# Rotary attention and dense experts on one core: the first pair's second queries rotated on GpSimd, its second keys turned two score tiles later, the third pair loaded sooner

## The chip, the cores and the metric

One core of a Trainium2 chip runs the whole kernel: five engines (TensorE, VectorE, ScalarE, GpSimd, and SyncE, which here only issues transfers) work on one program each and wait for one another by semaphores. In the rows TensorE is PE (its weight loads PEld), VectorE is DVE, ScalarE is ACT, GpSimd is POOL and SyncE is SP. The metric is the device time of one execution in microseconds (us), the median of the runs.

## What is computed

```python
def _attn_ref(q, k, v):                      # (2, 8, 576, 64) each
    ...
    def rotate(x):
        x1, x2 = (x[..., :half], x[..., half:])
        return np.concatenate([x1 * cos - x2 * sin, x1 * sin + x2 * cos], axis=-1)
    q_rot, k_rot = (rotate(q), rotate(k))
    scale = 1.0 / np.sqrt(D)
    scores = scale * np.matmul(q_rot, k_rot.transpose(0, 1, 3, 2))
    ...
    return np.matmul(attn, v)                # attn: softmax of the scores

def _moe_ref(x, domain_probs, w1, w2):       # x (1152, 512), 4 experts, all used by every token
    p = domain_probs / (domain_probs.sum(-1, keepdims=True) + 1e-09)
    for e in range(E):
        h = np.maximum(x @ w1[e], 0.0)
        out += p[:, e:e + 1] * (h @ w2[e])
```

Queries and keys are rotated, the softmax attention of 16 heads (2 batches, 8 heads) gives 1152 tokens of 512 features, and these go through four dense experts.

## The kernel before

All products are made of high and low halves in fp32r (a value and its rounding remainder), so every rotated tensor is split in two.

**Pairs and units.** Heads are worked two at a time, a pair: `first` holds the four pairs of batch 0, `second` those of batch 1. A pair's 2 x 576 queries make nine score tiles of 128 rows, the units u = 0 to 8: four of the pair's first head, four of its second, and one (`TAIL`) of the last 64 rows of both. For a unit TensorE makes a score tile `sc` (L281), VectorE takes its maximum `mx` (L292), ScalarE the exponential `e` (L300), TensorE turns `e` into `pp` (L314) and its end into `x` (L340), ScalarE and VectorE copy it as high and low part `ptH`, `ptL`, `ptX` (L331, L335, L343, L347), and every second unit TensorE multiplies with the values (L364 to L367). At a pair's end VectorE inverts the sums `total` (L381, L382), scales the last `e` (L386) and spreads the sums (`rep`, L391), which TensorE turns into `pr` (L397).

**What a pair needs first.** `load` brings raw keys, queries and values (SyncE queue, for the first pair's queries ScalarE's). `rotate` is six instructions on one engine: a product (L184), two half-width products (L188), their sum (L192), and the split into high part (L136 or L140) and low part (L141) of `hl`. `turn_heads` turns a head's rotated keys or queries on TensorE into a bank (`tpk`, `tpq`, L230), `keep_heads` copies the bank to `kT` or `qT` on ScalarE (L235), `turn_tails` and `keep_tails` do the last 64 rows (L253, L265), and `swap` makes the keys' other half `k2T` by two transfers (L245, L246). The first pair's first keys get `k2T` without a transfer.

**Banks.** Score tiles, and the turned heads unless another place is given, take the two `s` banks by turns: a tile can be written once the one before the last has been read.

**Order.** The program is in manual order: each engine runs its instructions as the Python code emits them. The first statements are emitted straight, the rest stands in `plan`, an agenda of due times in units: pair n begins at 9n, `ALONE` gives each step's offset, `FIRST_TURNS` and `TURNS` when the heads of the first and the next pair are turned and kept. Rotations of the third pair on are `jobs`: each half unit, `work(1)` emits one step of the oldest. After 44.5 units the experts of chunk 0 start, with batch 1's pairs between them, then the experts of chunk 1.

**Around the change.** The first pair's first head is rotated at once (keys on VectorE, queries on GpSimd). Then GpSimd rotates the second pair's keys and queries and splits its values, while VectorE rotates the first pair's second keys and then the second queries `pr.rotate("q", ...)` (256 columns, the split at 1.5 units). Buffers come from two pools by turns, `evens` for the first and third pair, `odds` for the second and fourth; the third pair's raw keys can be loaded once the first pair's have been read.

Of the kernel before, what the change touches and what calls it, by code (L numbers as in the profile page):

```python
# [15 lines left out]
F32R = mybir.dt.float32r  # L16
# [31 lines left out]
        tails=(5.299, 5.657), swap=5.707,  # L48
    ),
]  # L50
FIRST_TURNS = dict(q0=(1.327, 1.797), q1=(1.739, 1.84), q_tails=(-0.037, 0.16), swap=0.18)
NEXT_TURNS = dict(tails=(-0.01, -0.008), k=(0.03, 0.056), q=(0.975, 1.004))


# [1 line left out]
def kernel(  # L56
# [17 lines left out]
    nc = tc.nc  # L74
    B, H, S, D = q.shape
    NT, DM = out.shape
    E, _, FF = w1.shape
# [5 lines left out]
    NS = NR + 1  # L83
# [3 lines left out]
    NC = 2 * NR + 1  # L87
# [56 lines left out]
    class Pair:  # L144
# [60 lines left out]
        def turn(self, which, i):  # L205
            return self.hl[which][:, i].rearrange("p two d -> p (two d)")
# [250 lines left out]
    class Weights:  # L457
# [35 lines left out]
        def next(self):  # L493
            self.load()
            self.split()
# [126 lines left out]
    def dst(c, hp, a, z):  # L622
        return xH[c][:, hp, a:z], xL[c][:, hp, a:z]
# [6 lines left out]
    def pools(name, **kw):  # L630
        return [
            attn.enter_context(tc.tile_pool(name=f"{name}0", bufs=1, side="right", **kw)),
            spare.enter_context(tc.tile_pool(name=f"{name}1", bufs=1, **kw)),
        ]

    apool = attn.enter_context(tc.tile_pool(name="apool", bufs=1, side="right"))
    evens, odds = pools("pair")
    banks = {t: Banks(t, pools(t, space=PSUM)) for t in ("s", "pp")}
    banks["pt"] = Banks("pt", pools("pt"))
    xb = [p.tile([P, 512], F32, name=f"x{i}") for i, p in enumerate(pools("x", space=PSUM))]  # L640
# [4 lines left out]
    first = [  # L645
        Pair(0, hp, (evens, odds)[hp % 2], dst(0, hp, 0, SM), dst(1, hp, SM, S)) for hp in range(NP)
    ]
# [31 lines left out]
    plan = Agenda()  # L679
# [5 lines left out]
    def tails(t, pr, *args):  # L685
        plan.at(t[0], lambda: pr.turn_tails(*args))
        plan.at(t[1], lambda: pr.keep_tails(*args))


    pr, nx = first[0:2]  # L690
# [21 lines left out]
    pr.keep_heads("k", (0,), True)  # L712
    pr.keep_tails("k", True)
    pr.split_v(nc.scalar)
    nx.rotate_now("k", nc.gpsimd)
    nx.rotate_now("q", nc.gpsimd)
    nx.split_v()
    pr.rotate_now("k", nc.vector, NS, NC)
    rest = pr.rotate("q", nc.vector, NS, NC)
    for _ in range(3):  # L720
        next(rest)
    plan.at(1.5, lambda: next(rest))
    pr.turn_heads("k", (1,))
    pr.keep_heads("k", (1,))
    turn(FIRST_TURNS["q0"], pr, "q", (0,), False, (2, NR))
    turn(FIRST_TURNS["q1"], pr, "q", (1,))
    tails(FIRST_TURNS["q_tails"], pr, "q")
    plan.at(FIRST_TURNS["swap"], lambda pr=pr: pr.swap(1, 2))


    def load_qk(t, pr):
        def rotate():
            jobs.append(pr.rotate("k", nc.gpsimd))
            jobs.append(pr.rotate("q", nc.gpsimd))

        plan.at(t, lambda: pr.load("k"), lambda: pr.load("q"), rotate)

    def load_v(t, pr):
        plan.at(t, lambda: pr.load("v"), later(pr.split_v))
# [6 lines left out]
    for hp, pr in enumerate(first):  # L746
# [3 lines left out]
        if hp + 1 < NP:  # L750
# [5 lines left out]
                if key in t:  # L756
                    tails(shift(n, t[key]), nx, parts)
            plan.at(n + t["swap"], nx.swap)
    load_qk(7.2, first[2])
    load_v(U + 5.8, first[2])  # L760
    load_qk(U + 0.05, first[3])
    load_v(2 * U + 5.8, first[3])
# [92 lines left out]
```

## Time and profile before

| | |
|---|---|
| time, median of 3 runs | 593.22 us (590.82 to 593.9) |
| the profiled execution's own time | 592.81 us |
| its span, first to last instruction | 590.8 us |
| TensorE busy (matmul) | 559.1 us (95%) |
| VectorE, ScalarE, GpSimd busy | 236.3, 256.0, 279.4 us |
| mean granted TensorE clock | 0.993 |

Attention of batch 0 fills about the first 110 us of the span, the experts with batch 1's attention and then the experts alone the rest. The rows further down are from three views: the order of time (start, duration, engine, line, output<-input; in brackets the idle time before it and what ended it), and a table of stretches with TensorE's busy time and its granted clock, where 1.00 is the level of 2.4 GHz and 0.50 that of 1.2 GHz.

### The profile page before, as it was taken

Reading aid. Unit: us, or ns where it says so; the run is one execution under the profiler, and the core shown is the slowest. Engines: PE = TensorE matmul, PEld = TensorE weight load, DVE = VectorE, ACT = ScalarE, POOL = GpSimd, SP = SyncE. Lnnn points to the kernel's source line nnn. Section 1 sums busy time; section 2 is a strip of 40 time slices with the busy share of each in tenths; the row PEclk is TensorE's granted clock in tenths of the full one; section 3 lists DMA queues with packets and bytes.
Section 4 is the critical chain, followed back from the end, with each engine's and each line's share of the span. In section 5 each row is a group of like instructions: output and inputs, shape, how many; then the busy total and the mean of one; then the engine's idle time right before and its main releaser. Section 6 shows DMA issues by size and latency. Waiting matters only on the chain.

```text
span 590.8 us, 8478 instructions
## 1 busy us (share of the span) xinstructions
PE 559.1 (95%) x3325; PEld 493.6 (84%) x3325; DVE 236.3 (40%) x411; ACT 256.0 (43%) x505; POOL 279.4 (47%) x191
## 2 busy tenths in 40 slices
PE   3788889899999999999999999999999999999997
PEld 2677778688888888888888888998998899889985
DVE  6786889424363434444334542210321042022202
ACT  4685798365444545455535542331232133113300
POOL 7939993267933784378333343333334333333300
PEclk9998999899999999999999999999999999999999
DMA  5052232055126222432252113323222222322002
GB/s 153 15 156 69 71 99 59 0 150 182 36 72 175 71 65 54 124 119 65 72 134 73 60 52 112 96 82 100 71 73 72 71 72 73 101 76 72 0 1 89
DMA packets 40345, 48.57 MB, mean 82 GB/s; under 512 B 7154, under 2 KB 29938, under 8 KB 40306
## 3 DMA queue, kind: packets, MB, share of 16 engines
q1 hardware_dynamic: 39506, 47.28, 27.3%
q10 hardware_dynamic: 800, 0.75, 0.5%
q8 instruction: 26, 0.43, 0.3%
q14 instruction: 13, 0.11, 0.1%
HBM read 41.24 MB, written 2.36 MB: 74 GB/s over the span
## 4 chain that ended last, share of the span: by engine, by line
PE 82%; DVE 8%; ACT 5%; DMA 2%; issue 1%; POOL 1%; SPq 0%; ACTq 0%; DVEq 0%; POOLq 0%
PE po L546 11%; PE po L548 11%; PE po L547 11%; PE ph L567 11%; PE ph L568 11%; PE ph L569 11%; PE sc L281 5%; PE pp L314 4%; PE x L415 3%; ACT e L300 2%; DVE mx L292 2%; PE x L364 2%; PE x L365 2%; DMA rawk<-in_k_dram 1%; PE x L340 1%
## 5 line engine op out<-in xcount | busy, mean ns | idle before, releaser
L141 POOL TENSOR_TENSOR wl<-wr,wh 128x1024 fp32r<-128x1024 f32 x64 | 153.8, 2403 | 237.8 <-ACT wh L134 237.8
L567 PE MATMUL ph<-xH,wh 128*128 128x320 f32 (+1 forms) x384 | 130.6, 340 | 0.0
L569 PE MATMUL ph<-xH,wl 128*128 128x320 f32 (+1 forms) x384 | 129.3, 337 | 0.0
L568 PE MATMUL ph<-xL,wh 128*128 128x320 f32 (+1 forms) x384 | 129.2, 336 | 0.0
L546 PE MATMUL po<-wh,hH 128*128 128x512 f32 x288 | 114.6, 398 | 0.0
L134 ACT ACTIVATE wh<-wr 128x1024 fp32r<-128x1024 f32 x64 | 67.6, 1056 | 105.7 <-PE po L548 79.0
L548 PE MATMUL po<-wh,hL 128*128 128x512 f32 x288 | 112.5, 391 | 0.0
L547 PE MATMUL po<-wl,hH 128*128 128x512 f32 x288 | 112.4, 390 | 0.0
L532 DVE SCALAR_TENSOR_TENSOR hL<-ph,hH 128x320 fp32r<-128x320 f32 (+1 forms) x96 | 51.7, 558 | 145.4 <-ACT hH L531 145.4
L531 ACT ACTIVATE hH<-ph 128x320 fp32r<-128x320 f32 (+1 forms) x96 | 46.8, 491 | 109.1 <-PE ph L569 106.7
L569 PEld LDWEIGHTS ph<-xH,wl 128*128 128x128 f32 x384 | 72.1, 188 | 5.2
L567 PEld LDWEIGHTS ph<-xH,wh 128*128 128x128 f32 x384 | 72.1, 188 | 4.8
L568 PEld LDWEIGHTS ph<-xL,wh 128*128 128x128 f32 x384 | 72.2, 188 | 4.5
L292 DVE TENSOR_REDUCE mx<-sc 128x1 f32<-128x576 f32 x72 | 54.1, 752 | 38.8 <-PE sc L281 38.3
L300 ACT ACTIVATE e<-sc,mx 128x576 f32<-128x576 f32 x72 | 53.3, 740 | 27.4 <-DVE mx L292 26.7
L548 PEld LDWEIGHTS po<-wh,hL 128*128 128x128 f32 x288 | 54.1, 188 | 11.7
L546 PEld LDWEIGHTS po<-wh,hH 128*128 128x128 f32 x288 | 54.1, 188 | 11.2
L547 PEld LDWEIGHTS po<-wl,hH 128*128 128x128 f32 x288 | 54.2, 188 | 10.1
L577 DVE SCALAR_TENSOR_TENSOR acc<-po,probs,acc 128x512 f32<-128x512 f32 x27 | 18.8, 751 | 80.7 <-PE po L548 80.7
L314 PE MATMUL pp<-ident,e 128*128 128x128 f32 x288 | 45.3, 281 | 5.8 <-DVE e L386 3.0
L331 ACT ACTIVATE ptH<-pp 128x512 fp32r<-128x512 f32 x64 | 38.1, 595 | 27.2 <-PE x L364 17.0
L335 DVE TENSOR_TENSOR ptL<-pp,ptH 128x512 fp32r<-128x512 f32 x64 | 43.8, 685 | 9.6 <-ACT ptH L331 9.0
(103 smaller groups left out, 676.7 us busy)
## 6 DMA issues: line engine op xcount, KB each, us to landing
wr<-in_moe_w_dram SPq DMA_DIRECT2D x64, 512.0 KB, 3.5
k2T<-kT SPq DMA_DIRECT2D x14, 288.0 KB, 3.9
rawv<-in_v_dram SPq DMA_DIRECT2D x8, 256.0 KB, 2.9
out_dram<-acc SPq DMA_DIRECT2D x8, 256.0 KB, 3.2
rawk<-in_k_dram SPq DMA_DIRECT2D x7, 256.0 KB, 3.9
rawq<-in_q_dram SPq DMA_DIRECT2D x7, 256.0 KB, 3.1
rawv<-in_v_dram SPq DMA_DIRECT2D x16, 32.0 KB, 2.6
tabs<-in_rope_dram ACTq DMA_DIRECT2D x1, 320.0 KB, 3.5
```

The lines of the kernel that those rows point to most:

```text
L134: nc.scalar.activation(out=hi, in_=src, func=AF.Copy)
L141: eng_l.tensor_tensor(out=lo, in0=src, in1=f32(hi), op=ALU.subtract)
L292: nc.vector.tensor_reduce(out=mx, in_=self.sc[u][:, :, 0:HALF], op=ALU.max, axis=AX.XY, negate=True)
L300: nc.scalar.activation(out=e.rearrange("p (i c) -> p i c", i=2), in_=self.sc.pop(u)[:, :, 0:HALF], func=AF.Exp, bias=self.mx.pop(u), accum ...
L314: nc.tensor.transpose(pp[:, c * P : (c + 1) * P], self.e[u][:, c * P : (c + 1) * P], ident)
L532: nc.vector.scalar_tensor_tensor(out=tL[:, a:z], in0=o, scalar=0.0, in1=f32(tH[:, a:z]), op0=ALU.max, op1=ALU.subtract,)
L546: nc.tensor.matmul(po[t], lhsT=sH, rhs=wH, start=(f == 0), stop=False)
L547: nc.tensor.matmul(po[t], lhsT=sH, rhs=wL, start=False, stop=False)
L548: nc.tensor.matmul(po[t], lhsT=sL, rhs=wH, start=False, stop=(f == NF - 1))
L567: nc.tensor.matmul(o, lhsT=wH[:, kt], rhs=xh, start=(kt == 0), stop=False)
L568: nc.tensor.matmul(o, lhsT=wH[:, kt], rhs=xl, start=False, stop=False)
L569: nc.tensor.matmul(o, lhsT=wL[:, kt], rhs=xh, start=False, stop=(kt == KT1 - 1))
```

## The change

Three things are edited.

- The first pair's second queries (256 columns) are rotated on GpSimd, ahead of the second pair's keys, with the `odds` pool's scratch tiles, instead of on VectorE with those of `evens`. They are turned at 2.3 instead of 1.739 units and kept at 2.5 instead of 1.84.
- The first pair's second keys are turned at 1.1 and kept at 1.3 units, behind two score tiles, instead of ahead of the first; they go through the bank `xb[1]` and no longer through an `s` bank. Their swap is issued at 1.4 instead of 0.18 units. The third and fourth tiles of the first queries are kept at 1.45 instead of 1.797.
- The third pair's keys and queries are loaded, and their rotations queued, at 2.6 instead of 7.2 units.

```diff
-FIRST_TURNS = dict(q0=(1.327, 1.797), q1=(1.739, 1.84), q_tails=(-0.037, 0.16), swap=0.18)
+FIRST_TURNS = dict(q0=(1.327, 1.45), q1=(2.3, 2.5), q_tails=(-0.037, 0.16), swap=1.4)
...
     pr.split_v(nc.scalar)
+    pr.rotate_now("q", nc.gpsimd, NS, NC, odds)
     nx.rotate_now("k", nc.gpsimd)
     nx.rotate_now("q", nc.gpsimd)
     nx.split_v()
     pr.rotate_now("k", nc.vector, NS, NC)
-    rest = pr.rotate("q", nc.vector, NS, NC)
-    for _ in range(3):
-        next(rest)
-    plan.at(1.5, lambda: next(rest))
-    pr.turn_heads("k", (1,))
-    pr.keep_heads("k", (1,))
+    plan.at(1.1, lambda pr=pr: pr.turn_heads("k", (1,), tp=xb[1].bitcast(F32R).unsqueeze(1)))
+    plan.at(1.3, lambda pr=pr: pr.keep_heads("k", (1,)))
...
-    load_qk(7.2, first[2])
+    load_qk(2.6, first[2])
```

TensorE in the opening, before (`sc_0_0` is the first pair's score tile 0, `tpk_0` its second keys, `tpq_0` queries, first the third and fourth tiles of the first head, then the second head):

```order
L230 MATMUL tpk_0_238<-identr,hlk_00_149 128x128 x4
L281 MATMUL sc_0_0_245<-kT_0_185,qT_0_188 128x288 x2
L281 MATMUL sc_0_0_245<-k2T_0_197,qT_0_188 128x288 x2
L253 MATMUL tlq_00_250<-identr,hlq_00_158 128x128
L281 MATMUL sc_0_1_259<-kT_0_185,qT_0_188 128x288 x2
L281 MATMUL sc_0_1_259<-k2T_0_197,qT_0_188 128x288 x2
L230 MATMUL tpq_0_266<-identr,hlq_00_158 128x128 x2
L314 MATMUL pp_0_0_269<-ident,e_0_0_257 128x128 x4
L230 MATMUL tpq_0_281<-identr,hlq_00_158 128x128 x4
L281 MATMUL sc_0_2_287<-kT_0_185,qT_0_188 128x288 x2
```

and now (`x_113` is the bank `xb[1]`):

```order
L281 MATMUL sc_0_0_241<-kT_0_185,qT_0_188 128x288 x2
L281 MATMUL sc_0_0_241<-k2T_0_197,qT_0_188 128x288 x2
L253 MATMUL tlq_00_246<-identr,hlq_00_158 128x128
L281 MATMUL sc_0_1_253<-kT_0_185,qT_0_188 128x288 x2
L281 MATMUL sc_0_1_253<-k2T_0_197,qT_0_188 128x288 x2
L230 MATMUL x_113<-identr,hlk_00_149 128x128 x4
L230 MATMUL tpq_0_265<-identr,hlq_00_158 128x128 x2
L314 MATMUL pp_0_0_268<-ident,e_0_0_251 128x128 x4
L281 MATMUL sc_0_2_281<-kT_0_185,qT_0_188 128x288 x2
L281 MATMUL sc_0_2_281<-k2T_0_197,qT_0_188 128x288 x2
L340 MATMUL x_112<-ident,e_0_0_251 64x128
L230 MATMUL tpq_0_291<-identr,hlq_00_158 128x128 x4
```

The second keys moved from ahead of score tile 0 to behind tile 1, and the second queries from ahead of tile 2 to behind it.

ScalarE there, before:

```order
L235 ACTIVATE kT_0_185<-tpk_0_238 128x512
L265 ACTIVATE qTt<-tlq_00_250 128x2x64
L300 ACTIVATE e_0_0_257,total_0_244<-sc_0_0_245,mx_0_0_252 128x576
L300 ACTIVATE e_0_1_279,total_0_244<-sc_0_1_259,mx_0_1_264 128x576
L235 ACTIVATE qT_0_188<-tpq_0_266 128x256
L235 ACTIVATE qT_0_188<-tpq_0_281 128x512
L331 ACTIVATE ptH_0_0_274<-pp_0_0_269 128x4x128
L300 ACTIVATE e_0_2_303,total_0_244<-sc_0_2_287,mx_0_2_295 128x576
```

and now:

```order
L265 ACTIVATE qTt<-tlq_00_246 128x2x64
L300 ACTIVATE e_0_0_251,total_0_240<-sc_0_0_241,mx_0_0_248 128x576
L235 ACTIVATE kT_0_185<-x_113 128x512
L235 ACTIVATE qT_0_188<-tpq_0_265 128x256
L300 ACTIVATE e_0_1_279,total_0_240<-sc_0_1_253,mx_0_1_262 128x576
L331 ACTIVATE ptH_0_0_273<-pp_0_0_268 128x4x128
L235 ACTIVATE qT_0_188<-tpq_0_291 128x512
L300 ACTIVATE e_0_2_302,total_0_240<-sc_0_2_281,mx_0_2_288 128x576
```

Two copies now stand between the first two exponentials, and the copy of the second queries stands just ahead of the third.

GpSimd now (before, the five rows of `q_05` and `hlq_00` stood on VectorE, and `t1k_10` followed `vs_0`; `_10` is the second pair):

```order
L141 TENSOR_TENSOR vs_0_200<-rawv_0_129,vs_0_200 128x10x64
L184 TENSOR_TENSOR t1q_05_203<-rawq_0_124,tabs 128x256
L188 TENSOR_TENSOR t2q_05_204<-rawq_0_124,tabs 128x4x32 x2
L192 TENSOR_TENSOR t1q_05_203<-t1q_05_203,t2q_05_204 128x256
L136 TENSOR_SCALAR hlq_00_158<-t1q_05_203 128x4x64
L141 TENSOR_TENSOR hlq_00_158<-t1q_05_203,hlq_00_158 128x4x64
L184 TENSOR_TENSOR t1k_10_211<-rawk_1_133,tabs 128x576
```

Six instructions are put ahead of everything that GpSimd does for the later pairs; its order after that is the old one. On SyncE the six transfers of the third pair's keys and queries now stand right behind the first pair's swap, and before they stood behind the second pair's swap and the first load of weights. From the third pair on all engines keep their order.

## Rows read from the trace of the kernel before

**Rows 1.** Order of time, first pair's opening: VectorE, ScalarE, TensorE

```profile
11.63 1.65 DVE L184 TENSOR_TENSOR t1q<-rawq,tabs 128x256 f32<-128x256 f32 x1
...
16.35 1.41 DVE L292 TENSOR_REDUCE mx<-sc 128x1 f32<-128x576 f32 x2
...
17.13 0.74 ACT L300 ACTIVATE e<-sc,mx 128x576 f32<-128x576 f32 x1 [3.15 <-DVE mx L292]
...
18.01 0.49 PE L230 MATMUL tpq<-identr,hlq 128*128 128x128 f32 x2 [3.28 <-ACT e L300]
...
19.03 0.81 PE L230 MATMUL tpq<-identr,hlq 128*128 128x128 f32 x4
...
19.65 0.81 PE L281 MATMUL sc<-kT,qT 128*128 128x288 f32 x2
19.89 0.60 ACT L235 ACTIVATE qT<-tpq 128x512 fp32r<-128x512 f32 x1 [0.93 <-PE tpq L230]
...
21.66 0.83 PE L281 MATMUL sc<-kT,qT 128*128 128x288 f32 x2
...
23.37 0.51 PE L281 MATMUL sc<-kT,qT 128*128 128x288 f32 x2
```

**Rows 2.** Order of time, where TensorE turns later pairs' keys and queries

```profile
27.15 0.46 PE L230 MATMUL tpk<-identr,hlk 128*128 128x128 f32 x4
...
33.76 0.51 PE L230 MATMUL tpq<-identr,hlq 128*128 128x128 f32 x4
...
45.66 0.53 PE L230 MATMUL tpk<-identr,hlk 128*128 128x128 f32 x4 [2.29 <-POOL hlk L141]
...
52.85 0.25 PE L253 MATMUL tlkq<-identr,hlk 128*128 128x128 f32 x1
```

**Rows 3.** Table of stretches, TensorE: stretch, length, busy (matmuls), clock, DMA share, GB/s

```profile
47.00:48.00 1.00, 1.00 (x9) 0.50 0.08 16
```

**Rows 4.** Order of time, GpSimd's rotations and splits

```profile
7.82 0.73 POOL L184 TENSOR_TENSOR t1q<-rawq,tabs 128x192 f32<-128x192 f32 x1
...
10.73 0.59 POOL L141 TENSOR_TENSOR hlq<-t1q,hlq 128x192 fp32r<-128x192 f32 x1
...
11.33 1.67 POOL L141 TENSOR_TENSOR vs<-rawv,vs 128x640 fp32r<-128x640 f32 x1
...
20.11 1.41 POOL L184 TENSOR_TENSOR t1q<-rawq,tabs 128x576 f32<-128x576 f32 x1
...
25.37 1.44 POOL L141 TENSOR_TENSOR hlq<-t1q,hlq 128x576 fp32r<-128x576 f32 x1
...
38.50 1.42 POOL L184 TENSOR_TENSOR t1k<-rawk,tabs 128x576 f32<-128x576 f32 x1 [9.37 <-DVE ptL L335]
```

**Rows 5.** Order of time, TensorE between one pair's tail and the next's unit 5

```profile
32.37 0.51 PE L281 MATMUL sc<-kT,qTt 128*128 128x288 f32 x2
...
42.77 0.60 PE L397 MATMUL pr<-ident,rep 128*128 128x128 f32 x4
...
50.80 0.51 PE L281 MATMUL sc<-kT,qT 128*128 128x288 f32 x2
...
58.83 0.51 PE L281 MATMUL sc<-kT,qTt 128*128 128x288 f32 x2
...
69.88 0.60 PE L397 MATMUL pr<-ident,rep 128*128 128x128 f32 x4
...
70.34 0.51 PE L230 MATMUL tpk<-identr,hlk 128*128 128x128 f32 x4
...
74.36 0.51 PE L281 MATMUL sc<-kT,qT 128*128 128x288 f32 x2
```

**Rows 6.** Order of time, VectorE at two pairs' ends, and GpSimd beside it

```profile
35.82 0.17 DVE L381 TENSOR_SCALAR total<-total 128x9 f32<-128x9 f32 x1 [0.76 <-ACT e L300]
...
62.04 1.41 POOL L192 TENSOR_TENSOR t1q<-t1q,t2q 128x576 f32<-128x576 f32 x1
...
62.13 1.36 DVE L381 TENSOR_SCALAR total<-total 128x9 f32<-128x9 f32 x1
```

## The prediction

> **What bounds the kernel now.** The page's totals come first: TensorE's matmul row is busy in 95% of the span, so only a stretch in which it waits, or runs at its lower clock, can give time back. The chain of work and the order of time then show two such stretches in batch 0's attention, both fed by what is moved here.
>
> The first is the opening [rows 1]. VectorE begins the first pair's second queries at 11.63 and comes to the first maxima only at 16.35; two take 1.41, so one takes 0.70. ScalarE has by then waited 3.15 for its first exponential (17.13), and TensorE's wait for that ends at 18.01. Score tiles 2, 3 and 4 start at 19.65, 21.66 and 23.37. The pair of score products takes 0.83 at 21.66 and 0.51 at 23.37: TensorE rose from about half speed to full in between.
>
> The second is the third pair's keys [rows 2]: TensorE waits 2.29 for GpSimd's `hlk` and turns them at 45.66. GpSimd had been idle for 9.37 before it began on them at 38.50 [rows 4], because the load had been issued late. After that wait TensorE's granted clock is 0.50, the 1.2 GHz level [rows 3].
>
> **The change part by part.** *GpSimd's new work.* No row has a rotation of 256 columns on GpSimd. The nearest are 192 columns, 7.82 to 11.32 = 3.50, and 576 columns, 20.11 to 26.81 = 6.70 [rows 4]; these are the two bounds. I take the straight line between them, 3.50 + (64/384) x 3.20 = 4.0, as 256 lies next to 192. It starts when the values' low half is done: 11.33 + 1.67 = 13.0 [rows 4], about 12.9 without VectorE's own rotation beside it. So the second queries are ready at about 16.9. Behind them GpSimd does the old work later by 3.7 (4.0 less some 0.3 that the same rotation beside it no longer costs): the second pair's keys at 23.7 instead of 20.0, its queries at 30.5 instead of 26.8, its values' split at 32.8 instead of 29.1.
>
> *The opening.* VectorE's rotation goes, so its first maximum can start when the second keys are done: 11.65 instead of 16.35. With 0.70 for it and some 0.1 to ScalarE the first exponential runs at 12.45, 4.7 sooner. ScalarE then copies the second keys and two query tiles (0.60 for a full head [rows 1], some 0.4 for half of one), so the second exponential runs at 14.2 and score tile 2, which needs its bank, at 15.1 instead of 19.65: 4.55 sooner. Here a part is given back. The second queries wait for GpSimd until 16.9; their turning takes 0.8 and their copy 0.5 before the next starts [rows 1], and the third exponential is queued behind that copy on ScalarE: 18.3, and done at 19.2. Score tile 3 needs the bank of that exponential, because the second queries' tile took the other one, so it starts at 19.2 instead of 21.66: 2.45 sooner. In the old run tiles 3 and 4 lie 1.71 apart at mostly half speed. If TensorE has risen by 19, 0.35 is saved there: **2.8 sooner** in all. If it rises at 22.7 as before, the gain shrinks to about 2.0, and if already at 15, it is about 3.1. The second keys' turning costs nothing: it lies in TensorE's wait for the first exponential. Their swap is issued at about 13.9 instead of 13.1, and score tile 4, the first that needs it, comes at 20.6.
>
> *Does GpSimd hold it up?* TensorE wants the second pair's keys at 27.15 - 2.8 = 24.35 and they are ready at 23.7; it wants the queries at 33.76 - 2.8 = 30.95 and they are ready at 30.5 [rows 2]. The cover is thin: 0.65 and 0.45. So GpSimd caps the opening's gain at about 3.3.
>
> *The load.* SyncE issues the third pair's six transfers right behind the first swap. The keys' buffer has been read by VectorE before 11.63 [rows 1]; the queries' buffer is read by GpSimd's new rotation until about 15, so SyncE waits there, and behind it stand only the probabilities and the second pair's swap, which can't start before that pair's keys are turned (27.15 before, 24.35 now). Both tensors land long before GpSimd is free at 32.8, so the load is no longer a term. GpSimd rotates the keys from 32.8 to about 39.7 instead of 38.50 to 45.6, and the queries until 46.5. The 9.37 of idleness takes up the added 3.7.
>
> *The second stretch* is priced by the same stretch one pair later, in which GpSimd never pauses [rows 5]. From the tail's score tile to the next pair's unit 5 it takes 50.80 - 32.37 = 18.43 here and 74.36 - 58.83 = 15.53 there: **2.9**. The parts agree. The wait is 2.29. The clock: from the turning of the keys to unit 5 it is 50.80 - 45.66 = 5.14 after the wait and 74.36 - 70.34 = 4.02 at full speed, 1.12. Against them stands GpSimd's company: with GpSimd idle the second pair's divisor set-up on VectorE takes 0.17, beside GpSimd's addition the same takes 1.36 and ends with it [rows 6]. From the tail's score tile to the turning of the sums TensorE needs 42.77 - 32.37 = 10.40 with GpSimd idle and 69.88 - 58.83 = 11.05 beside it, so 0.65. The sum is 2.29 + 1.12 - 0.65 = 2.76, and 0.14 stays unnamed. TensorE would arrive at the keys at 43.37 - 2.8 + 0.65 = 41.2, and they are there at 39.7: the wait goes whole. What is next is the third pair's queries: wanted at 52.85 - 5.7 = 47.15, ready at 46.5.
>
> The Trainium skill (SBUF — State Buffer, section "Who interferes with whom") says that VectorE and GpSimd share one pair of SBUF ports and that the one which comes second is blocked for the other's whole instruction. The trace agrees: the 1.36 ends with GpSimd's 1.41 [rows 6]. By that rule the price is no fixed 0.65 but hangs on where in GpSimd's instruction VectorE comes; rival C works that out from rows.
>
> *After unit 5* of the second pair every engine's order is the old one and all loads come earlier. TensorE is the busiest engine there, so the gain is carried to the end, give or take 0.6 at each later pair's end, where the same blocking falls differently.
>
> **Sum.** Against the profiled execution's own 592.81 (span 590.8): 592.8 - 2.8 - 2.9 = 587.1. The median of the runs lies 0.4 above it, so 587.5.
>
> **Rivals.** *B: GpSimd becomes the bound.* If its 256 columns cost the upper bound, 6.7, the second pair's queries come at 33.2 and the opening gains 0.55 of 2.8. The third pair's keys come at 42.4, when TensorE arrives at about 43.5, so the 2.9 stays: 593.2 - 3.45 = 589.8. For it: the cover of 0.45. Against it: the 192-column row is much the nearer.
>
> *C: the blocking costs more.* At a pair's end three VectorE instructions of this kind follow each other (L381, L386, L391). If each comes just behind a GpSimd start, they wait up to 1.4 each, 4.2 instead of 0.65, and the gain falls to 5.7 - 3.55 = 2.15: 591.1, within what can be told from no change. That the freed stretch at the keys is only half regained (the change not doing what it says) ends at about the same time. Against it: the stretch one pair later carries three such waits and still takes only 15.53.
>
> *D: slower.* TensorE stays at the lower level through the new opening and beyond it, as it did in the old one until after 21.66. At that level the same work takes 5.14/4.02 = 1.28 as long [rows 5], so each us of it costs 0.28. What remains of the gain is then 2.0 + 2.9 = 4.9, used up after 17.5 us of work, that is if the level lasts to about 45; it is slower by 0.5% if it lasts to about 59: 596.2. For it: it did fall after the wait at 45.66 [rows 3]. Against it: the old run rose between 21.66 and 23.37, after it took up work at 18.01, and the new one waits less and takes up the same work 4.5 sooner.
>
> **How the numbers follow.** The forecast has 0.62, B 0.16, C 0.16, D 0.06. The forecast's own range goes from 585.5 (opening 3.3, second stretch 3.5 with the clock kept and little blocking, 0.9 from the median's scatter) to 589.3. The range of 8 in 10 adds B and most of C above: 585.2 to 591.0. About 0.5% (3.0 us) can be told from no change, so faster means under 590.25: the forecast and B, 0.78. C is the same, 0.16. D is slower, 0.06.
>
> **What would show it.** Right: the first exponential at about 12.5 and score tile 3 at about 19.2; a GpSimd without a pause from 5 to beyond 60; no wait for `hlk` at the third pair's keys and no granted clock of 0.50 after it; unit 5 of the second pair at about 45 instead of 50.80. Wrong: TensorE waiting for GpSimd's `hlk` or `hlq` at the second pair (B), VectorE's three small instructions at the first pair's end taking several us (C), score products of 0.8 beyond 23 (D). The forecast would also be wrong if the pace of the later pairs, or the end of attention, gave the gain back.

## The result, and the profile of the changed kernel

The changed kernel takes 587.27 us (median of 5 runs, 586.28 to 587.85); the kernel before, on the same chip, takes 592.96 us (5 runs, 590.82 to 593.9). The ratio is 0.9911, 95% interval 0.9883 to 0.9938: 5.7 us faster. The forecast was 587.5. The profiled execution of the changed kernel took 586.44, its span is 584.2.

The page of the changed kernel, its totals:

```profile
span 584.2 us, 8482 instructions
...
PE 559.1 (96%) x3325; PEld 492.9 (84%) x3325; DVE 231.2 (40%) x405; ACT 256.1 (44%) x505; POOL 282.5 (48%) x197
```

TensorE's busy time is the 559.1 it was, in a span 6.6 shorter: by the totals, what went away is waiting. What the clock gave back can't be read from them, only from the stretches below. VectorE has 5.1 less and GpSimd 3.1 more, which is the rotation that changed engines.

The opening of the changed kernel, in order of time (start, length, engine, line; in brackets the wait just ahead and what ended it); it answers to [rows 1]:

```profile
12.37 0.74 ACT L300 ACTIVATE e<-sc,mx 128x576 f32<-128x576 f32 x1 [0.24 <-DVE mx L292]
...
13.04 0.72 POOL L184 TENSOR_TENSOR t1q<-rawq,tabs 128x256 f32<-128x256 f32 x1
...
15.04 0.85 PE L281 MATMUL sc<-kT,qT 128*128 128x288 f32 x2 [0.42 <-ACT e L300]
...
15.97 0.74 POOL L141 TENSOR_TENSOR hlq<-t1q,hlq 128x256 fp32r<-128x256 f32 x1
...
18.05 0.73 ACT L300 ACTIVATE e<-sc,mx 128x576 f32<-128x576 f32 x1
...
18.92 0.85 PE L281 MATMUL sc<-kT,qT 128*128 128x288 f32 x2 [0.54 <-ACT e L300]
...
20.97 0.83 PE L281 MATMUL sc<-kT,qT 128*128 128x288 f32 x2
...
22.86 0.51 PE L281 MATMUL sc<-kT,qT 128*128 128x288 f32 x2
```

ScalarE's wait of 3.15 for the first maxima is 0.24. The first exponential comes 4.76 sooner and score tile 2 4.61 sooner. Then the second queries, finished by GpSimd at 15.97 + 0.74 = 16.71, hold the third exponential until 18.05, and tile 3 is only 2.74 sooner. A pair of score products takes 0.83 at 20.97 and 0.51 at 22.86: TensorE came up to full speed at about the time it did before.

The second stretch, all engines, from the first pair's tail to the second pair's unit 5; it answers to [rows 2], [rows 5] and the first row of [rows 6]:

```profile
29.90 0.51 PE L281 MATMUL sc<-kT,qTt 128*128 128x288 f32 x2
...
33.34 0.63 DVE L381 TENSOR_SCALAR total<-total 128x9 f32<-128x9 f32 x1 [0.74 <-ACT e L300]
...
38.03 1.62 POOL L141 TENSOR_TENSOR hlk<-t1k,hlk 128x576 fp32r<-128x576 f32 x1
...
40.38 0.60 PE L397 MATMUL pr<-ident,rep 128*128 128x128 f32 x4
...
40.83 0.51 PE L230 MATMUL tpk<-identr,hlk 128*128 128x128 f32 x4
...
44.48 0.51 PE L281 MATMUL sc<-kT,qT 128*128 128x288 f32 x2
```

GpSimd has the third pair's keys ready at 39.65, TensorE turns them at 40.83, and the row has no wait. Its granted clock there (stretch, length, busy time and matmuls, clock, DMA share, GB/s):

```profile
42.00:46.00 4.00, 4.00 (x37) 1.00 0.26 77
```

It is full, where [rows 3] read 0.50. Unit 5 starts at 44.48 instead of 50.80.

The lead of the changed kernel over the one before, by the start of the same instruction in both profiled executions:

| place | before | after | lead |
|---|---|---|---|
| first exponential | 17.13 | 12.37 | 4.76 |
| score tile 2 | 19.65 | 15.04 | 4.61 |
| score tile 3 | 21.66 | 18.92 | 2.74 |
| score tile 4 | 23.37 | 20.97 | 2.40 |
| first pair's tail tile | 32.37 | 29.90 | 2.47 |
| third pair's keys turned | 45.66 | 40.83 | 4.83 |
| second pair's unit 5 | 50.80 | 44.48 | 6.32 |
| third pair's unit 0 | 62.15 | 55.00 | 7.15 |
| fourth pair's unit 0 | 84.31 | 76.18 | 8.13 |
| fourth pair's unit 1 | 86.63 | 80.21 | 6.42 |
| first matmul of the experts | 112.94 | 106.37 | 6.57 |
| last instruction (span) | 590.8 | 584.2 | 6.6 |

Two steps behind unit 5 were not in the sum: up by 1.81 between the second pair's unit 7 and the third pair's unit 3, down by 1.71 at the fourth pair's first two tiles. Changed kernel, order of time:

```profile
48.86 0.50 DVE L127 TENSOR_TENSOR probs<-probs,ptot 128x36 f32<-128x36 f32 x1
...
54.98 0.36 DVE L381 TENSOR_SCALAR total<-total 128x9 f32<-128x9 f32 x1
...
76.16 0.97 DVE L381 TENSOR_SCALAR total<-total 128x9 f32<-128x9 f32 x1
...
77.07 2.36 POOL L141 TENSOR_TENSOR wl<-wr,wh 128x1024 fp32r<-128x1024 f32 x1
...
77.42 2.33 DVE L386 TENSOR_SCALAR e<-e,total 128x576 f32<-128x576 f32 x1
...
79.80 0.66 PE L314 MATMUL pp<-ident,e 128*128 128x128 f32 x4 [1.64 <-DVE e L386]
```

and the kernel before at three of these instructions:

```profile
55.53 1.24 DVE L127 TENSOR_TENSOR probs<-probs,ptot 128x36 f32<-128x36 f32 x1
...
82.95 2.37 POOL L141 TENSOR_TENSOR wl<-wr,wh 128x1024 fp32r<-128x1024 f32 x1
...
85.64 0.52 DVE L386 TENSOR_SCALAR e<-e,total 128x576 f32<-128x576 f32 x1
```

Of the 1.81, 0.59 stands at the second pair's tail tile: just ahead of its unit 7's maximum VectorE divides the expert probabilities (L127), which took 1.24 and ended with an addition of GpSimd (55.29 + 1.42 = 56.71), and now takes 0.50. Another 0.71 stands at the third pair's unit 1: L381 at the third pair's start takes 0.36 instead of the 1.36 of [rows 6]; it now comes into a half-width product of GpSimd (54.53, 0.80 long) and ends with that. At the fourth pair it is the other way round. There L386, the scaling of the tail's probabilities, starts 0.35 behind GpSimd's subtraction for a half of the weights (2.36) and takes 2.33; before, that subtraction was over at 85.32 and L386 took 0.52. TensorE waits 1.64 for it.

### The profile page after: what moved, and what is told of

The parts are those of the page before. It is cut to its first block, busy times and chain, and to the rows that moved or that the text cites. A ratio compares the mean times of both kernels' runs of the same rounds, so it can differ in the third digit from the quotient of the medians.

```text
span 584.2 us, 8482 instructions
## 1 busy us (share of the span) xinstructions
PE 559.1 (96%) x3325; PEld 492.9 (84%) x3325; DVE 231.2 (40%) x405; ACT 256.1 (44%) x505; POOL 282.5 (48%) x197
## 3 DMA queue, kind: packets, MB, share of 16 engines
HBM read 41.24 MB, written 2.36 MB: 75 GB/s over the span
## 4 chain that ended last, share of the span: by engine, by line
PE 85%; ACT 5%; DVE 5%; DMA 2%; issue 1%; SPq 1%; POOL 1%; ACTq 0%; POOLq 0%
PE po L546 11%; PE po L548 11%; PE po L547 11%; PE ph L567 11%; PE ph L569 11%; PE ph L568 11%; PE sc L281 6%; PE pp L314 4%; ACT e L300 2%; PE x L415 2%; PE x L364 2%; PE x L365 2%; DVE mx L292 1%; PE x L340 1%; DVE total L381 1%
```

## The experiments

The theory: the gain is two separate terms, the opening (set by GpSimd's second queries and by when TensorE rises) and the second stretch (the wait for the third pair's keys, and the clock after it). What comes later is where VectorE's small instructions fall against GpSimd's long ones. The rivals: the two terms are one (the load alone, or the opening alone, gives all); GpSimd is already the bound; the collisions set the end. The first four kernels share one chip and its runs of the kernel before (median 592.73), the last four another (591.91).

**The load alone.** The kernel before, with only the load moved.

```diff
-    load_qk(7.2, first[2])
+    load_qk(2.6, first[2])
```

> The kernel before with the third pair's keys and queries loaded at 2.6 units and nothing else. My theory (the second stretch is its own term): the opening stays as before (first exponential at 17.13, score tile 4 at 23.37), GpSimd goes on to the third pair's keys at about 29.2 instead of 38.50, TensorE's wait of 2.29 for them and the half-speed stretch after it go, and the second pair's unit 5 starts 3 to 4 us sooner than 50.80. Time 588.5 to 590, a gain of 3 to 4. Rival (the load helps only once GpSimd's and TensorE's opening are moved too): unit 5 moves by under 1 us and the time stays above 592.

Measured: 588.97 (7 runs, 587.73 to 589.13), ratio 0.9929, interval 0.9903 to 0.9955, 3.8 sooner. TensorE, order of time:

```profile
43.65 0.51 PE L230 MATMUL tpk<-identr,hlk 128*128 128x128 f32 x4
...
47.30 0.51 PE L281 MATMUL sc<-kT,qT 128*128 128x288 f32 x2
```

The opening is the old one (score tile 4 at 23.25, tail tile at 32.01). The wait at the keys is gone, and from there to unit 5 it is 3.65, as in the changed kernel. Unit 5 comes 3.5 sooner than in [rows 5], of which 0.36 was there at the tail tile. So the load is a term of its own.

**The opening alone.** The changed kernel, with the load put back.

```diff
-    load_qk(2.6, first[2])
+    load_qk(7.2, first[2])
```

> The changed kernel with the third pair's load put back to 7.2 units. My theory: the opening's lead of 2.4 to 2.5 us is kept up to the third pair's keys, the wait of about 2.3 for them and the lower clock behind it come back, since the load is issued sooner by the same lead only. Time about 590.4 (gain 2.5), and together with the load alone the parts add up to the whole change. Rival (the wait swallows the opening's lead, because the keys come when they came before): the third pair's keys are turned at 45.7 as before, the time stays within 0.5 of the kernel before.

Measured: median 590.39 (10 runs), ratio 0.9946, interval 0.9913 to 0.9979, 2.3 sooner. The ten runs lie in two groups, three from 584.95 to 586.64 and seven from 590.18 to 592.85, and the only trace (585.54) is of the first. In that trace GpSimd and TensorE, then TensorE's stretch after the wait:

```profile
40.73 1.41 POOL L141 TENSOR_TENSOR hlk<-t1k,hlk 128x576 fp32r<-128x576 f32 x1
...
42.19 0.53 PE L230 MATMUL tpk<-identr,hlk 128*128 128x128 f32 x4 [1.74 <-POOL hlk L141]
```

```profile
46.00:48.00 2.00, 2.00 (x20) 1.00 0.44 129
```

The wait is back, 1.74, as it should be without the earlier load; but the clock after it is 1.00, where the same kind of wait was followed by 0.50 in [rows 3]. Unit 5 is at 45.85, 4.95 sooner than before and 1.37 later than in the changed kernel. The two parts' medians add up: 3.8 + 2.3 = 6.1 against 5.7. But the three runs gain 6.1 to 7.8 with the opening alone, as much as both parts together, so the sum of the parts holds for the medians only. The record has each run's mean granted clock: 0.996 to 1.000 in the three, 0.987 to 0.993 in the seven. The slower group spent more of its time at the lower clock; whether it fell after that wait can't be read, since the group has no trace.

**TensorE at work from the start.** To see whether an earlier rise is to be had, 40 transposes of the identity stand ahead of all work.

```diff
+    for _ in range(40):
+        nc.tensor.transpose(xb[0].bitcast(F32R)[:, 0:P], identr, identr)
```

> The changed kernel with 40 more transposes of the identity on TensorE at the very start, into a bank that is written over later; they lie in its idle time before 8 us. In the changed kernel the score products still take 0.83 at 20.97 and 0.51 from 22.86, so the rise of the clock came no sooner than in the kernel before, and the step of my prediction that put it at 19 failed. If the work done before decides when TensorE rises, these transposes bring it forward to 15 or sooner, score tile 4 starts at about 20.5 instead of 20.97 and tile 5 0.5 to 0.8 sooner than 22.86, and the time falls by 0.4 to 0.8. Rival (the rise comes at about 22.5 whatever TensorE did): no difference in durations before 22 and none in the time.

Measured: 587.7 (5 runs, 587.15 to 588.68), ratio 0.9916: no gain, where 0.4 to 0.8 was expected. TensorE, order of time and then stretches:

```profile
1.94 5.14 PE L656 MATMUL x<-identr 128*128 128x128 f32 x40 [1.94 <-DVE identr L104]
...
8.29 0.53 PE L230 MATMUL tpk<-identr,hlk 128*128 128x128 f32 x4 [1.21 <-DVE hlk L141]
...
9.95 0.80 PE L281 MATMUL sc<-kT,qT 128*128 128x288 f32 x2 [0.45 <-ACT qT L235]
...
21.05 0.83 PE L281 MATMUL sc<-kT,qT 128*128 128x288 f32 x2
```

```profile
8.00:12.00 4.00, 3.03 (x18) 0.75 0.64 185
12.00:16.00 4.00, 3.58 (x17) 0.50 0.27 63
...
20.00:24.00 4.00, 4.00 (x20) 0.54 0.08 9
24.00:28.00 4.00, 3.66 (x31) 1.00 0.00 0
```

TensorE was up at 8.29 (0.53 for four transposes) and down again for the score products at 9.95 (0.80); then it rose at the end of the stretch from 20 to 24, a little later than in the changed kernel. In this execution a rise made ahead of the opening's waits didn't outlast them.

**The second queries behind tile 3.** The third exponential no longer queues behind the copy of the second queries, which are turned one tile later and through the spare bank.

```diff
-    turn(FIRST_TURNS["q1"], pr, "q", (1,))
+    plan.at(2.82, lambda pr=pr: pr.turn_heads("q", (1,), tp=xb[1].bitcast(F32R).unsqueeze(1)))
+    plan.at(2.95, lambda pr=pr: pr.keep_heads("q", (1,)))
```

> The changed kernel with the second queries turned behind score tile 3 (2.82 units) through the bank of the second keys and copied at 2.95, so that they take no score bank and stand behind the third exponential. It tests the step which said that bank and copy give back 2.1 us at score tile 3. My theory: tile 3 starts at about 17.3 instead of 18.92, tile 4 at about 20 instead of 20.97, and the lead grows by 0.7 to 1.1, until GpSimd's queries of the second pair (wanted 1.1 sooner at most) stop it; time lower by about 0.8. Rival (at half speed TensorE itself is the bound there): tile 3 comes sooner but tile 5 does not, and the time is the changed kernel's within 0.3.

Measured: 584.04 (4 runs, 582.79 to 584.49), ratio 0.9848, interval 0.981 to 0.9885: some 3.7 better than the changed kernel by the two ratios, whose intervals just touch; by the two spans it is 584.2 - 582.1 = 2.1. TensorE, order of time:

```profile
15.08 0.53 PE L281 MATMUL sc<-kT,qT 128*128 128x288 f32 x2 [0.69 <-ACT e L300]
...
16.18 0.51 PE L281 MATMUL sc<-kT,qT 128*128 128x288 f32 x2
...
23.54 0.54 PE L230 MATMUL tpk<-identr,hlk 128*128 128x128 f32 x4 [1.35 <-POOL hlk L141]
...
30.32 0.53 PE L230 MATMUL tpq<-identr,hlq 128*128 128x128 f32 x4 [0.93 <-POOL hlq L141]
```

Tile 3 is 2.74 sooner than in the changed kernel, tile 4 (18.07) 2.9 sooner; in this execution TensorE is already at full speed at 15.08. So the clock has part in it: in the last kernel below, which has the same edit but 0.85 at tile 2 and 0.83 at tile 3, tiles 3 and 4 are 1.91 and 1.47 sooner (17.01 and 19.50). Then GpSimd is the bound, as the prediction had it: TensorE waits 1.35 and 0.93, and the second pair's queries are turned 33.76 - 30.32 = 3.44 sooner than in [rows 2] (the cap was put at 3.3). Over the changed kernel 0.75 is left at unit 5 of the second pair; 1.3 more comes at the fourth pair, whose tiles 0 and 1 lie 2.71 apart (75.48 and 78.19) instead of 4.03, because L386 (76.19) now stands behind another, shorter instruction of GpSimd (75.97, 1.44 long) and takes 1.52.

**Without one small instruction.** L381 adds 1e-9 to sums that are at least 1; this kernel leaves that addition out.

```diff
-            nc.vector.tensor_scalar_add(self.total, self.total, 1e-9)
```

> The changed kernel without the addition of 1e-9 to the sums (L381) at each pair's end. In the changed kernel TensorE waits 1.64 at 79.80 and 1.93 at 100.30 for VectorE's scaling of the last exponential (L386), which stood behind GpSimd: first L381 0.97, then L386 2.33, ending with GpSimd's weight half (2.36). My theory: this wait is what took 1.7 us of the lead at the fourth pair's beginning, and it hangs on the moment. Without L381 the scaling starts about 1 us sooner, ahead of the weight half that begins at 77.07, and takes about 0.5; the third pair's end gets 1.5 to 1.9 back and the last pair's end 1, so 585 or a little less. Rival (TensorE's lead is lost to something else there): unit 1 of the fourth pair stays 4.0 behind unit 0 and the time stays within 0.5 of the changed kernel.

Measured: 582.05 (4 runs, 580.65 to 583.35), ratio 0.9847, interval 0.981 to 0.9884, some 3.8 better than the changed kernel by the ratios, whose intervals just touch. All engines at the fourth pair, order of time (the file has a line less, so L386 reads L385):

```profile
76.82 0.98 DVE L385 TENSOR_SCALAR e<-e,total 128x576 f32<-128x576 f32 x1
...
77.43 2.61 POOL L141 TENSOR_TENSOR wl<-wr,wh 128x1024 fp32r<-128x1024 f32 x1
```

The scaling now gets in ahead of GpSimd's subtraction and takes 0.98 instead of 2.33; tiles 0 and 1 of that pair lie 2.18 apart (76.58 and 78.76). The first matmul of the experts starts at 104.23, 2.1 sooner. The span is 3.1 shorter; the other 1.0 lies in the experts: from their first matmul to the end it is 476.9 here, 476.0 in the last kernel below, which has no addition either, and 477.7 to 478.0 in the eight others. Batch 1's pairs, worked between the experts, have the addition too: in the changed kernel it takes up to 1.75 there, and TensorE's waits in the 450 us behind that first matmul come to some 1.6; here they come to 0.8, in the last kernel to none.

**GpSimd made longer.** Four more instructions of the rotation, of some 2.35 in all and with a result that nothing uses, ahead of the second pair's keys.

```diff
     pr.rotate_now("q", nc.gpsimd, NS, NC, odds)
+    more = pr.rotate("q", nc.gpsimd, NS, NC, odds)
+    for _ in range(3):
+        next(more)
```

> The changed kernel with four more GpSimd instructions of 256 columns (a repeated half of the rotation, about 2.35 us) ahead of the second pair's keys, whose result nobody uses. It measures GpSimd's cover. In the changed kernel the second pair's keys are done at 23.45 and turned at 24.66, the queries done at 30.2 and turned at 31.27, the third pair's keys done at 39.65 and turned at 40.83: 1.1 to 1.2 each. My theory: the first 1.1 to 1.2 cost nothing, the rest costs one for one, so TensorE waits about 1.2 at the second pair's keys and the lead at the second pair's unit 0 falls from 2.5 to about 1.3; afterwards no more is lost, and the time is about 1.2 higher, 588.5, give or take what falls otherwise at the later pairs' ends. Rival (GpSimd had more cover, or the score tiles were the bound): the lead at unit 0 falls by under 0.4.

Measured: 586.21 (4 runs, 585.91 to 586.78), ratio 0.992, interval 0.9889 to 0.995: no slower than the changed kernel, where 1.2 more was expected. All engines, order of time:

```profile
25.76 0.54 PE L230 MATMUL tpk<-identr,hlk 128*128 128x128 f32 x4 [1.28 <-POOL hlk L141]
...
32.55 0.54 PE L230 MATMUL tpq<-identr,hlq 128*128 128x128 f32 x4 [0.89 <-POOL hlq L141]
...
78.40 1.53 DVE L386 TENSOR_SCALAR e<-e,total 128x576 f32<-128x576 f32 x1
79.55 2.60 POOL L141 TENSOR_TENSOR wl<-wr,wh 128x1024 fp32r<-128x1024 f32 x1
```

The mechanism of rival B is there: GpSimd holds TensorE twice, and the lead over the kernel before is 36.21 - 35.04 = 1.17 at the second pair's unit 0, 1.3 less than in the changed kernel. At the fourth pair's unit 0 it is still 1.53 behind. But everything behind that comes later by as much, L386 falls otherwise and takes 1.53 instead of 2.33, and at unit 1 only 0.18 is left; the experts start at 106.24 against 106.37. A loss on the path was given back by a collision.

**The second queries' rotation on VectorE, later.** Is GpSimd needed, or would it do to put the rotation behind the first two maxima on its old engine?

```diff
-    pr.rotate_now("q", nc.gpsimd, NS, NC, odds)
...
+    rest = pr.rotate("q", nc.vector, NS, NC)
+    for i in range(4):
+        plan.at(1.15 + 0.05 * i, lambda: next(rest))
```

> The changed kernel with the second queries' rotation left on VectorE, but put behind its first two maxima; all the rest is as changed, and GpSimd goes straight on to the second pair. It asks whether the move to GpSimd is needed or only that the maxima come first. My theory: VectorE rotates from 13.7 to about 18.5 (5.9 beside GpSimd in the kernel before, 4 alone), the third maximum waits for that until about 18.5 instead of 16.4, score tile 3 starts at 20.5 to 21 instead of 18.92, and the opening's lead is about 1 instead of 2.5; the wait for the third pair's keys is away all the same, so the time is 588 to 589. Rival (the order alone is what counts): the lead is 2.5 as in the changed kernel and the time within 0.5 of it.

Measured: 588.75 (10 runs, 586.39 to 590.54), ratio 0.9949, interval 0.9929 to 0.9969. VectorE and TensorE, order of time:

```profile
13.81 1.28 DVE L184 TENSOR_TENSOR t1q<-rawq,tabs 128x256 f32<-128x256 f32 x1
...
19.00 1.58 DVE L141 TENSOR_TENSOR hlq<-t1q,hlq 128x256 fp32r<-128x256 f32 x1
20.50 0.74 DVE L292 TENSOR_REDUCE mx<-sc 128x1 f32<-128x576 f32 x1
...
20.72 0.72 PE L230 MATMUL tpq<-identr,hlq 128*128 128x128 f32 x4 [4.48 <-DVE hlq L141]
```

Beside GpSimd's own work the rotation takes VectorE 20.58 - 13.81 = 6.8, where GpSimd took 3.67. The third maximum queues behind it, TensorE waits 4.48, and the tail tile starts at 34.33, 1.96 later than in the kernel before, where a lead of about 1 was expected. What this kernel has over the kernel before is not the opening's: unit 5 of the second pair is 1.93 ahead, 3.89 more than the tail tile, which is the load's term, and the experts start 4.74 ahead (108.20). Of that, 1.5 comes behind the last score tile, where the clock stays up in this execution and fell in the one of before. So the time met its expectation in part by luck.

**All three.** The later second queries (edit as above), no addition, and the scaling of L386 on ScalarE.

```diff
-            nc.vector.tensor_scalar_add(self.total, self.total, 1e-9)
...
-            nc.vector.tensor_scalar_mul(e, e, self.total[:, TAIL:])
+            nc.scalar.activation(out=e, in_=e, func=AF.Copy, scale=self.total[:, TAIL:])
```

> The changed kernel with three edits together: the second queries turned behind score tile 3 through the bank of the second keys, no addition of 1e-9 (L381), and the scaling of each pair's last exponential (L386) on ScalarE instead of VectorE, where GpSimd can't stand ahead of it. My theory: the opening gains until TensorE waits for GpSimd at the second pair's keys and queries (0.8 to 1 us net), and the pair ends no longer hang on the moment; experts start at about 103.5 instead of 106.37 and the time is 583 to 584. Rival (ScalarE is put into the chain by it: it waits for VectorE's reciprocal with the next exponential behind it): each pair's end costs 0.3 to 0.5 more, and the time is no lower than that of the run with the queries behind tile 3, 584.0.

Measured: 580.68 (4 runs, 580.5 to 580.8), ratio 0.9825, interval 0.979 to 0.9861: better than the changed kernel, whose interval begins at 0.9883. The last pair's end, ScalarE and TensorE here:

```profile
96.10 0.78 ACT L385 ACTIVATE e<-e,total 128x576 f32<-128x576 f32 x1 [0.28 <-DVE total L381]
...
96.93 0.66 PE L314 MATMUL pp<-ident,e 128*128 128x128 f32 x4 [0.64 <-ACT e L385]
```

and in the changed kernel:

```profile
100.30 0.63 PE L314 MATMUL pp<-ident,e 128*128 128x128 f32 x4 [1.93 <-DVE e L386]
```

The wait there falls from 1.93 to 0.64, because VectorE's addition (L381), which took 1.40 there, is gone. From the last score tile to the experts it is 102.34 - 92.80 = 9.54 instead of 106.37 - 94.90 = 11.47, but most of these 1.93 is the clock. The changed kernel's TensorE in that stretch (table of stretches), then the last pair's end in the kernel with the rotation on VectorE (order of time):

```profile
100.00:105.00 5.00, 4.37 (x24) 0.66 0.00 0
```

```profile
103.49 0.63 PE L314 MATMUL pp<-ident,e 128*128 128x128 f32 x4 [1.92 <-DVE e L386]
```

The second of them has the changed kernel's pair end, the same wait and a clock of 1.00, and needs 108.20 - 98.07 = 10.13; two others like it need 10.15 (the opening alone) and 10.16 (TensorE at work from the start). So some 0.6 is the edits' (what is saved at one wait is in part lost at the next, 1.00 instead of 0.33) and 1.3 the clock. The mean granted clock is 0.998 to 1.000 in all four runs of this kernel and 0.987 to 0.996 in the changed kernel's five; that the edits keep it up is not shown. The gains don't add: two edits are worth some 3.8 each alone, and all three together 5.1 by the ratios. Both had taken the same collision at the fourth pair; that this is the whole reason is not shown.

## Why the prediction was right, point by point

**The sum** held: 5.7 forecast, 5.69 by the medians; that it did so to 0.01 is luck. By the traces the terms come to somewhat more, 6.3 at unit 5 and 6.6 at the end: the profiled execution of the changed kernel lies 0.83 under its median, that of the kernel before 0.15. Two terms were off, in opposite directions (-0.3 and +0.95), and two later steps, missing from the sum, cancelled to 0.1.

**The opening**, forecast 2.8, measured 2.40 to 2.49. The chain of the steps was met within 0.3: first exponential 12.37 (12.45 forecast), tile 2 15.04 (15.1), second queries 16.71 (16.9), third exponential 18.05 (18.3), tile 3 18.92 (19.2). GpSimd's 256 columns cost 3.67, so the value of 4.0 was 0.33 high and the row of 192 columns the right neighbour. The step that failed is the rise: it was put ahead of 19 and came between 20.97 and 22.86. Tiles 3 and 4 lie 2.05 apart, 0.34 more than the 1.71 of before, where 0.35 was to be saved; so tile 3's 2.74 became 2.40. The bound named for that case, 2.0, and the 0.28 by which tile 3 was sooner than forecast come near this.

**GpSimd's cover** was thin and held: no wait stands at the second pair's keys and queries. It was 1.21 and 1.03 (turned at 24.66 and 31.27, ready at 23.45 and 30.24) where 0.65 and 0.45 were forecast. That it is thin, and that it caps the gain at about 3.3, was right: 2.35 more work on GpSimd cost 1.3 there, and a faster opening stopped at 3.44.

**The second stretch**, forecast 2.9, measured 18.43 - (44.48 - 29.90) = 3.85. The mechanism was right: the wait of 2.29 goes whole, the load was the cause (the load alone does it), and the clock stays up. The term that was mis-sized is GpSimd's company. From the tail tile to the turning of the sums it is 40.38 - 29.90 = 10.48; forecast 11.05, with GpSimd idle 10.40. So GpSimd's company costs TensorE 0.08 there and not 0.65, which is 0.57 of the 0.95: L381 does take 0.63 instead of 0.17, but TensorE doesn't wait for what follows from it. The other 0.37 lies behind the keys: 44.48 - 40.83 = 3.65 instead of the 4.02 of the pair that served as the model.

**After unit 5** the forecast was "carried to the end, give or take 0.6 at each later pair's end". That bound failed: the steps were +1.81 and -1.71. The cause was right (small instructions of VectorE against GpSimd's long ones) and so was most of the place (L381 and L386); L127, worth 0.59, was not thought of. The size was taken from one pair, in which only the instructions of a rotation, up to 1.4 long, stood in the way; the halves of the weights, 2.36 long, were not thought of. The rule of the Trainium skill (SBUF — State Buffer, section "Who interferes with whom"), that whichever of VectorE and GpSimd first has the pair of ports that they share holds it for its whole instruction and the other is blocked, agrees: L386 starts 0.35 behind the 2.36 and takes 2.33. L381 at 33.34 comes late in GpSimd's 1.41 that began at 32.52, ends with it, and takes 0.63. The price is what is left of the other's instruction, so it hangs on a few tenths of phase.

**Rivals.** B (GpSimd the bound) is not what happened, but lies some 1.0 away: that is what the opening can still gain before TensorE waits (3.44 - 2.47). C's mechanism is real at the fourth pair, with one instruction of 2.33 and not three at the first pair's end. D didn't happen: score products of 0.51 from 22.86 on, and 1.00 from 42 to 46. Its price was read wrongly: the 5.14 of [rows 5] was at 0.50 only in part (its mean granted clock is 0.67), so 1.28 is too low for work at that level; the same score products take 0.83 at the lower level and 0.51 at the higher [rows 1], 1.6 times as long.

## What to carry to other kernels

A late load that makes the matmul engine wait is worth the wait and, where one follows, the slower clock after it, and both can be read from one stretch of the trace before; another execution may not have the slower clock. Work that is moved to an engine with idle time costs only what that idle time doesn't cover; work out when each later consumer wants its input, since the cover caps every further gain. Where two engines block each other, don't carry a saving past the next meeting point unchanged: take the longest instruction that can stand in the way there, on both sides, as the bound. Before a difference between two traces is put down to an edit, compare the clock of the two stretches.

## What the runs showed of the hardware that was not expected

- TensorE's rise in the opening is not the same in each execution of nearly the same work. With tile 2 at 15.04 and 15.08 and the same work ahead of it, its products took 0.85 in the changed kernel and 0.53 in the kernel with the later second queries. Of the eight traces with the new opening, four have 0.53 or 0.54 at tile 2; three of these are back at 0.85 at tile 3, behind waits for the second queries, and only the kernel with the later second queries, which has no such wait, keeps its rise.
- A rise made early need not last: 40 transposes brought TensorE up by 8.29, and it was down by 9.95, after a wait of 1.21 and one of 0.45.
- A wait of 1.74 was followed by a clock of 1.00 in one execution (the opening alone), a wait of 2.29 by 0.50 in another [rows 3].
- Behind the last score tile of batch 0's attention the clock fell in some executions and not in others (0.66 from 100 to 105 in the changed kernel). With the same instructions from there to the experts, five traces in which it fell take 11.18 to 11.64, three in which it read 1.00 take 10.13 to 10.16.
- Until the first change of level is recorded, the clock of a stretch reads 1.00 whatever it is: in the changed kernel it does so from 20 to 22, where a pair of score products takes 0.83. In such a stretch the level is read from the length of the same matmul, 0.83 or 0.51.
- A rotation of 256 columns takes GpSimd 3.67 and VectorE 6.8 beside a working GpSimd (5.8 in the opening of before: 4.7 from 11.63 to the maxima at 16.35, and 1.1 for the split behind them).
